# GpSimd in place of SyncE as issuer of the 16-row query and key copies in the first three units

## The chip, the cores and the metric

The kernel runs on one core of one Trainium2 chip. The metric is the device time of one execution in microseconds (us). Five engines work side by side, each through its own instructions in order: TensorE (PE; its weight loads are shown as PEld), VectorE (DVE), ScalarE (ACT), GpSimd (POOL) and SyncE (SP). They wait for each other by semaphores. An engine that issues a DMA hands the copy to the 16 DMA engines and goes on; the time that the issue itself takes on SP is shown as SPq.

## The reference

Three stages follow each other. A linear attention with a complex decay, per head, for 4 batches, 8 heads, 768 positions and a head width of 48:

```python
a_re_n, a_im_n = (a_re * scale, a_im * scale)       # scale = min(|a|, 0.999) / (|a| + 1e-6)
for t in range(S):
    new_re = ar * S_re - ai * S_im
    new_im = ar * S_im + ai * S_re
    S_re, S_im = (new_re + kv, new_im)              # kv = outer(k[t], v[t])
    y[:, :, t] = einsum('bhd,bhde->bhe', q[:, :, t], S_re)
```

Its output, 3072 tokens of 384 channels, goes through a dense layer `g = h * cos(h)` with `h = x @ w_in` and `g @ w_out` (2048 hidden channels), and then through a mixture of 8 experts of 1024 hidden channels: each token goes to the expert with the largest logit, and the result is scaled by two gates.

## The kernel before

The sequence is cut into chunks of 128 positions, and two chunks make a **unit**; there are 12 units (0 to 11). For each unit three things happen, pipelined over the units.

- **Scan** (`scan`, L377 and after). DVE forms the running products of the decay in `core` (tiles `t`, `l_t`, `pb`), their inverse in `inverse`, and normalises the next unit's decay in `normal` (the last large step is the product on `a_t`). `gates` is a run of small GpSimd instructions on `fg`, `eb` and `ne`.
- **`post`** multiplies queries and keys with the decay (`qkt`, in two parts r = 0 and 1, real and imaginary) and then brings them from the layout of the scan, channels over all 128 partitions, into the layout of the matmuls, 48 rows for each head and part: `out_` does it with five DMAs for each chunk and part into the tile `qkr`, all issued by SyncE: two copies of 48 rows (L372, heads 0 to 5), one of 32 rows (L373) and two of 16 rows (L375). The last three belong to heads 6 and 7, whose 48 channels lie in two places. A unit has two chunks and two parts, so 12 + 8 = 20 DMAs. At their end SP issues the load of the next `qk_t` (L229).
- **`attn`** computes the scores from `qkr` (PE L444, tile `sc`), masks them on DVE (`pt`), and adds the state: `s_` and its copy `ss` with the two halves swapped, which two more DMAs of SP make (L491, L492). `s_` and `ss` are multiplied with a column of `qkr` for all heads and added into `tp`; `pv_t` (L463, L468) gives the chunk's output, and `x` is its copy for the dense layer. The next chunk's state comes from PE `m` (L481).

The dense layer is `mm1` (L513), the cosine on ACT and DVE (`act2`, `act3`) and `mm2` (L577), eight steps for each unit; `evac`, `routing` and GpSimd's indirect scatters (L585) bring each token's row to its expert. In units 0 and 1 the weights of the dense layer are still being decoded, checked and multiplied (L706 to L755), on DVE, ACT and PE. After the last unit comes the mixture of experts, which is mostly PE.

A scheduler sets the order of each engine's instructions: it takes the program, simulates it with its own durations, and places what it believes ready first, by priority. So who issues a DMA changes not only that queue but also the order on the other engines. For each DMA the copies into `qkr` are told apart by region: scores of heads 0 to 3 wait for the 48-row copies alone, while the products `s_` and `ss` need the copies of all heads of their chunk in both parts.

Of the kernel before, what the change touches and what calls it, by code (L numbers as in the profile page):

```python
# [140 lines left out]
def build(tc, ap, out, force=False):  # L141
    nc = tc.nc
    V, A, G, PE, SY = nc.vector, nc.scalar, nc.gpsimd, nc.tensor, nc.sync
# [66 lines left out]
    def tt(e, o, a, b, op):  # L210
        return e.tensor_tensor(out=o, in0=a, in1=b, op=op)  # L211
# [16 lines left out]
    def load_qk(u):  # L228
        SY.dma_start(qk_t, ap["qk"][u])  # L229
# [129 lines left out]
    def put_gates():  # L359
        bc = [128, 2, NCOL, 2]  # L360
        A.copy(qkt[:, :, :, :, C], fg[:, 2, 0:1].unsqueeze(3).to_broadcast(bc))
        A.copy(qkt[:, :, :, :, C + 1], fg[:, 0].unsqueeze(3).to_broadcast(bc))

    def post(u):
        qkr_t[u] = [qkrp.tile([96, H, 2, QP], F32, name="qkr") for _ in range(UC)]

        def out_(cc, r):

            s = qkt[:, r, 3 * cc:3 * cc + 3].rearrange("p j k t -> p j (k t)")
            d = qkr_t[u][cc][48 * r:48 * r + 48].rearrange("d h k t -> d h (k t)")  # L370
            for i in range(2):
                SY.dma_start(d[:, i:6:2], s[48 * i:48 * i + 48])  # L372
            SY.dma_start(d[0:32, 6:8], s[96:128, 0:2])  # L373
            for i in range(2):
                SY.dma_start(d[32:48, 6 + i], s[96 + 16 * i:112 + 16 * i, 2])  # L375

        nc_ = UC if u < 1 else 1  # L377
        put_gates()
        for cc in range(nc_):
            c = slice(NCOL // nc_ * cc, NCOL // nc_ * (cc + 1))  # L380
            for r in range(2):
                n = NCOL // nc_
                mark["post", u] = tt(V, qkt[:, r, c, :, 0:C].rearrange("p c k t -> p k c t"),
                                     l_t[:, r:r + 1, c].to_broadcast([128, 2, n, C]), qk_t[:, :, c], MUL)
                yield
                for k in [cc] if nc_ == UC else range(UC):
                    out_(k, r)
        if u + 1 < NU:
            load_qk(u + 1)
        yield  # L390
# [872 lines left out]
    if True:  # L1263
# [34 lines left out]
        for u in range(NU):  # L1298
# [21 lines left out]
            for s in range(NS):  # L1320
# [6 lines left out]
                i = u * NS + s - 2  # L1327
# [60 lines left out]
```

## Time and profile before

| | us |
|---|---|
| median of 3 runs | 952.21 (951.52 to 952.86) |
| the profiled execution | 952.07 |
| its span on the core | 950.3 |
| PE busy | 867.6 |
| DVE busy | 659.0 |
| ACT busy | 571.8 |
| POOL busy | 142.0 |

The profile gives for each engine its instructions in order with start and duration, what ended the idle time ahead of them, and the chain of work that ended last. The profiled execution is 1.8 us longer than its span, which is time around the program on the core. From about 600 us on PE has hardly a gap; the units 0 to 2 lie in the first 215 us, where no engine is busy all the time.

### The profile page before, as it was taken

Reading aid. Unit: us, or ns where it says so; the run is one execution under the profiler, and the core shown is the slowest. Engines: PE = TensorE matmul, PEld = TensorE weight load, DVE = VectorE, ACT = ScalarE, POOL = GpSimd, SP = SyncE. Lnnn points to the kernel's source line nnn. Section 1 sums busy time; section 2 is a strip of 40 time slices with the busy share of each in tenths; the row PEclk is TensorE's granted clock in tenths of the full one; section 3 lists DMA queues with packets and bytes.
Section 4 is the critical chain, followed back from the end, with each engine's and each line's share of the span. In section 5 each row is a group of like instructions: output and inputs, shape, how many; then the busy total and the mean of one; then the engine's idle time right before and its main releaser. Section 6 shows DMA issues by size and latency. Waiting matters only on the chain.

```text
span 950.3 us, 18853 instructions
## 1 busy us (share of the span) xinstructions
PE 867.6 (91%) x7149; PEld 758.8 (80%) x7149; DVE 659.0 (69%) x1416; ACT 571.8 (60%) x1264; POOL 142.0 (15%) x246
## 2 busy tenths in 40 slices
PE   0477989979999799999999999899999999999997
PEld 0456677757777588888878889789899899999997
DVE  6988878887877698989888888444564454345521
ACT  7684976647665758676767766445764354355521
POOL 0000101021111222311312021101111110212111
PEclk9997999999999999999999999999999999999999
DMA  9813046337265544241415450341337552454100
GB/s 332 329 44 97 30 109 217 102 113 208 70 173 175 158 133 131 63 129 53 139 52 153 136 172 19 104 140 50 96 103 220 171 181 59 137 186 145 29 28 28
DMA packets 67206, 119.13 MB, mean 125 GB/s; under 512 B 12239, under 2 KB 44895, under 8 KB 66836
## 3 DMA queue, kind: packets, MB, share of 16 engines
q1 hardware_dynamic: 60132, 107.75, 36.5%
q0 software_dynamic: 6976, 10.10, 3.2%
q8 instruction: 58, 0.95, 0.4%
q14 instruction: 40, 0.33, 0.1%
HBM read 80.69 MB, written 26.77 MB: 113 GB/s over the span
## 4 chain that ended last, share of the span: by engine, by line
PE 40%; DVE 23%; ACT 13%; DMA 9%; issue 7%; SPq 6%; POOL 1%; DVEq 0%; ACTq 0%; POOLq 0%
PE h L965 10%; PE o L577 6%; PE h L513 6%; PE p L989 6%; PE p L981 4%; DVE qkt L211 4%; DVE t L211 3%; DMA qkr<-qkt 3%; DVE l_t L211 2%; DVE g L561 2%; SPq L375 2%; SPq L372 2%; DVE nt L211 2%; PE sc L444 2%; DVE pt L211 2%
## 5 line engine op out<-in xcount | busy, mean ns | idle before, releaser
L513 PE MATMUL h<-x,wi 128*128 128x256 f32 x1728 | 243.7, 292 | 10.5 <-DVE g L561 6.3
L513 PEld LDWEIGHTS h<-x,wi 128*128 128x128 f32 x1728 | 218.2, 192 | 25.3 <-DVE g L561 7.7
L577 PE MATMUL o<-wo,g 128*128 128x400 f32 x464 | 169.4, 505 | 1.9 <-DVE g L561 1.9
L577 PEld LDWEIGHTS o<-wo,g 128*128 128x128 f32 x464 | 83.6, 191 | 53.4 <-issue 2.7
L965 PE MATMUL h<-xe,w1t 128*128 128x384 f32 (+6 forms) x576 | 118.7, 349 | 0.0
L969 DVE SCALAR_TENSOR_TENSOR hh<-h,hh 128x384 fp32r<-128x384 f32 (+6 forms) x64 | 37.2, 582 | 117.5 <-ACT hh L968 117.5
L965 PEld LDWEIGHTS h<-xe,w1t 128*128 128x128 f32 x576 | 101.9, 188 | 5.2
L968 ACT ACTIVATE hh<-h 128x384 fp32r<-128x384 f32 (+6 forms) x64 | 32.8, 514 | 114.1 <-PE h L965 108.9
L521 ACT ACTIVATE g<-h 128x512 f32<-128x512 f32 x96 | 57.3, 597 | 52.0 <-PE h L513 52.0
L561 DVE SCALAR_TENSOR_TENSOR g<-g,h 128x512 f32<-128x512 f32 x96 | 65.4, 681 | 31.6 <-ACT g L523 31.4
L585 POOL DMA_INDIRECT xs<-rows,si x46 | 60.0, 1305 | 177.9 <-DVE si L632 58.1
L989 PE MATMUL p<-w2t,hh 128*128 128x384 f32 (+1 forms) x384 | 76.7, 343 | 0.0
L577 PE MATMUL o<-wo,gh 128*128 128x400 f32 x304 | 69.4, 350 | 0.0
L989 PEld LDWEIGHTS p<-w2t,hh 128*128 128x128 f32 (+1 forms) x384 | 66.0, 186 | 1.5 <-ACT hh L968 0.4
L523 ACT ACTIVATE g<-g 128x512 f32<-128x512 f32 x96 | 60.8, 633 | 2.1
L444 PE MATMUL sc<-qkr 96*128 96x128 f32 x384 | 56.1, 288 | 5.5 <-ACT rows L601 2.7
L522 ACT ACTIVATE g<-h 128x512 f32<-128x512 f32 x96 | 57.9, 603 | 1.8
L444 PEld LDWEIGHTS sc<-qkr 96*128 96x128 f32 x384 | 51.1, 199 | 9.7 <-issue 3.7
L211 POOL TENSOR_TENSOR fg<-l_t,m 128x12 f32<-128x12 f32 x24 | 5.9, 268 | 350.9 <-DVE l_t L211 236.2
L585 POOL DMA_INDIRECT out_dram<-o,tok x28 | 34.6, 1234 | 150.2 <-issue 56.1
L577 PEld LDWEIGHTS o<-wo,gh 128*128 128x128 f32 x304 | 53.3, 188 | 0.5
L555 ACT CAST gh<-g 128x512 fp32r<-128x512 f32 x38 | 23.4, 617 | 44.2 <-DVE g L561 44.1
(290 smaller groups left out, 1562.7 us busy)
## 6 DMA issues: line engine op xcount, KB each, us to landing
stg<-in_w_dram SPq DMA_DIRECT2D x32, 768.0 KB, 6.3
qkr<-qkt SPq DMA_DIRECT2D x96, 146.2 KB, 3.4
a_t<-in_a_dram SPq DMA_DIRECT2D x12, 768.0 KB, 5.3
qk_t<-in_qk_dram SPq DMA_DIRECT2D x12, 768.0 KB, 4.9
xs<-in_xz_dram SPq DMA_DIRECT2D x17, 401.0 KB, 8.2
vt<-in_v_dram SPq DMA_DIRECT2D x24, 256.0 KB, 2.6
raw<-in_w_in_dram SPq DMA_DIRECT2D x7, 768.0 KB, 12.9
raw<-in_w_out_dram SPq DMA_DIRECT2D x7, 768.0 KB, 15.8
```

The source lines that it names most:

```text
L211: return e.tensor_tensor(out=o, in0=a, in1=b, op=op)
L444: PE.matmul(sc[:, h], lhsT=t[:, h, 1, 0:C], rhs=t[:, h, 0, 0:C], start=True, stop=True)
L513: PE.matmul(h[:, i], lhsT=wis[s][:, wi, kk, i * 128:(i + 1) * 128], rhs=x_t[u][:, xi, kk], start=n == 0, stop=n == 8)
L521: A.activation(out=g, in_=h, func=AF.Square, accum_out=hck[:, u * NS + s:u * NS + s + 1])
L522: mark["sin"] = A.activation(out=g, in_=h, func=AF.Sin, scale=0.5)
L523: A.activation(out=g, in_=g, func=AF.Square, scale=float(np.sqrt(2.0)))
L561: V.scalar_tensor_tensor(out=g, in0=g, scalar=1.0, in1=hps.pop((u, s)), op0=SUB, op1=MUL)
L577: PE.matmul(o, lhsT=a[:, i, cs], rhs=w[:, i], start=s == 0 and n == 0 and i == 0, stop=s == NS - 1 and n == len(prods) - 1 and i == 1)
L585: sc = G.indirect_dma_start(in_offset=None, oob_is_err=False, **kw)
L965: PE.matmul(h, lhsT=w[:, wi, kk, f * 128:(f + 1) * 128], rhs=x[:, xi, kk], start=n == 0, stop=n == 8)
L981: PE.matmul(o2[e][d][:, 0:c], lhsT=w[:, wi, f, d * 128:(d + 1) * 128], rhs=hh[:, hi], start=f == 0 and n == 0, stop=f == KE - 1 and n == 2)
L989: mm = PE.matmul(o2[e][j][0:w_, 0:DM], lhsT=hh[:, hi, j * w_:(j + 1) * w_], rhs=w[:, wi, f], start=f == 0 and n == 0, stop=f == KE - 1 and ...
```

## The change

In units 0 to 2 the copies of 16 rows (L375) are issued by GpSimd; in units 3 to 11 SyncE goes on issuing them.

```diff
             for i in range(2):
-                SY.dma_start(d[32:48, 6 + i], s[96 + 16 * i:112 + 16 * i, 2])
+                (G if u < 3 else SY).dma_start(d[32:48, 6 + i], s[96 + 16 * i:112 + 16 * i, 2])
```

That is 8 DMAs for each of three units, 24 in all. On SyncE, here in unit 0, the end of the copies before (from the last chunk and part on):

```order
L372 DMA qkr<-qkt 48x3x260 x2
L373 DMA qkr<-qkt 32x520
L375 DMA qkr<-qkt 16x260 x2
L229 DMA qk_t<-in_qk_dram 128x1536
L491 DMA ss<-s__468 48x384
```

and now on GpSimd, between the gates of unit 0 (`fg`) and those of unit 1:

```order
L356 TENSOR_SCALAR fg<-fg 128x6
L357 COPY fg<-fg 128x6
L375 DMA qkr<-qkt 16x260 x8
L211 TENSOR_TENSOR fg<-l_t,m_131 128x12 x2
L348 COPY eb<-l_t 128x2x6
```

SP now goes from L373 to the next L372, or to L229, at once; nothing else stands between GpSimd's gates and the eight copies.

The order on the other engines moved with it. On PE in unit 0, from the transposes of keys on (`sc` are scores from `qkr`, `m` the state of the next chunk), before:

```order
L429 MATMUL m<-ident,qkt 128x128 x3
L481 MATMUL m<-vt,kn 32x48 x19
L444 MATMUL sc<-qkr 128x128 x2
L481 MATMUL m<-vt,kn 32x48 x4
L444 MATMUL sc<-qkr 128x128 x4
L481 MATMUL m<-vt,kn 32x48
L444 MATMUL sc<-qkr 128x128 x2
L481 MATMUL m<-vt,kn 32x48 x24
```

and now:

```order
L429 MATMUL m<-ident,qkt 128x128 x3
L444 MATMUL sc<-qkr 128x128 x6
L481 MATMUL m<-vt,kn 32x48 x8
L444 MATMUL sc<-qkr 128x128 x2
L481 MATMUL m<-vt,kn 32x48 x16
L444 MATMUL sc<-qkr 128x128 x4
```

The scores of chunk 0 moved ahead of its state; the third row from the end of the second list, two scores of heads 6 and 7, needs GpSimd's copies, and 16 matmuls of the state stand behind it.

On ACT, between the inverse of unit 2 (L250, L254, L255, L243) and its gates (L361), before:

```order
L254 ACT_TABLE_LOAD
L254 ACTIVATE qkt<-nt 128x768
L523 ACTIVATE g<-g 128x512
L255 ACTIVATE qkt<-qkt 128x768
L243 ACTIVATE a_t<-nt 128x768
L521 ACTIVATE g,hck<-h 128x512
L522 ACT_TABLE_LOAD
L522 ACTIVATE g<-h 128x512
L523 ACTIVATE g<-g 128x512
L361 COPY qkt<-fg 128x24
```

and now:

```order
L254 ACT_TABLE_LOAD
L254 ACTIVATE qkt<-nt 128x768
L601 ACTIVATE rows<-o_1069 128x400
L522 ACT_TABLE_LOAD
L522 ACTIVATE g<-h 128x512
L255 ACTIVATE qkt<-qkt 128x768
L243 ACT_TABLE_LOAD
L243 ACTIVATE a_t<-nt 128x768
L601 ACTIVATE rows<-o_1070 128x400
L523 ACTIVATE g<-g 128x512
L521 ACTIVATE g,hck<-h 128x512
L361 COPY qkt<-fg 128x24
```

A sine of the dense layer (L522) moved in between the functions of the inverse, and the table of functions is loaded twice more: once ahead of L243, and once more behind L361, where the next row is again a load for L522. On DVE the products of the state also moved ahead: in unit 1 `s_` with `ss` stands now ahead of the product on `a_t` and stood behind it, and in unit 2 it stands ahead of the first products `t` of the next scan, where five instructions of that scan stood ahead of it.

## Rows read from the trace of the kernel before

**Rows 1.** The page's part 4: the chain that ended last, by line.

```profile
PE h L965 10%; PE o L577 6%; PE h L513 6%; PE p L989 6%; PE p L981 4%; DVE qkt L211 4%; DVE t L211 3%; DMA qkr<-qkt 3%; DVE l_t L211 2%; DVE g L561 2%; SPq L375 2%; SPq L372 2%; DVE nt L211 2%; PE sc L444 2%; DVE pt L211 2%
```

**Rows 2.** Busy time in stretches: stretch, its length, busy us (instructions), clock, DMA.

```profile
122.00:150.00 28.00, 25.63 (x354) 22.04 (x354) 20.71 (x47) 17.70 (x52) 0.00 (x0) 0.94 0.42 110
150.00:172.00 22.00, 21.68 (x130) 17.21 (x130) 17.25 (x33) 18.12 (x36) 3.01 (x14) 1.00 0.60 213
...
360.00:405.00 45.00, 45.00 (x452) 39.18 (x451) 40.05 (x86) 31.92 (x75) 12.86 (x20) 1.00 0.36 106
```

**Rows 3.** Timeline of SP: start, us, engine, line, operation, tiles, count.

```profile
62.13 1.39 SPq L372 DMA_DIRECT2D qkr<-qkt  x2
...
64.21 1.22 SPq L375 DMA_DIRECT2D qkr<-qkt  x2
...
75.43 0.58 SPq L229 DMA_DIRECT2D qk_t<-in_qk_dram  x1
76.11 0.51 SPq L491 DMA_DIRECT2D ss<-s__468  x1
...
121.76 1.29 SPq L372 DMA_DIRECT2D qkr<-qkt  x2
...
171.15 1.33 SPq L372 DMA_DIRECT2D qkr<-qkt  x2
```

**Rows 4.** The chain in order of time, 55 to 215 us: start, us, what.

```profile
76.67 5.08 DMA ss<-s__468
```

**Rows 5.** Timeline of PE; in brackets the idle time ahead and what ended it.

```profile
85.13 0.65 PE L463 MATMUL pv_t<-qkr,tp 96*32 96x128 f32 x8 [5.77 <-DVE tp L211]
...
131.81 0.68 PE L444 MATMUL sc<-qkr 96*128 96x128 f32 x4 [0.41 <-DMA qkr<-qkt]
```

**Rows 6.** Timeline of DVE in units 0 to 2.

```profile
64.59 1.02 DVE L706 TENSOR_SCALAR raw<-raw 128x768 uint32<-128x768 uint32 x2
...
75.28 0.68 DVE L211 TENSOR_TENSOR pt<-sc,cb 128x512 f32<-128x512 f32 x1
...
80.06 0.96 DVE L211 TENSOR_TENSOR wi<-raw,wi 128x768 fp32r<-128x768 f32 x1 [1.56 <-ACT wi L727]
81.93 0.56 DVE L211 TENSOR_TENSOR s__468<-s__468,qkr 96x384 f32<-96x384 f32 x1 [0.91 <-DMA ss<-s__468]
...
129.56 1.76 DVE L211 TENSOR_TENSOR a_t<-a_t,nt 128x1536 f32<-128x1536 f32 x1
...
133.38 0.56 DVE L211 TENSOR_TENSOR s__549<-s__549,qkr 96x384 f32<-96x384 f32 x1 [0.87 <-DMA qkr<-qkt]
...
141.93 0.56 DVE L211 TENSOR_TENSOR s__888<-s__888,qkr 96x384 f32<-96x384 f32 x1 [1.31 <-DMA ss<-s__888]
...
180.21 0.63 DVE L211 TENSOR_TENSOR t<-a_t 128x192 f32<-128x192 f32 x2 [1.67 <-ACT a_t L291]
...
183.38 0.56 DVE L211 TENSOR_TENSOR s__969<-s__969,qkr 96x384 f32<-96x384 f32 x1 [1.50 <-DMA qkr<-qkt]
```

**Rows 7.** Timeline of GpSimd: indirect scatters, later in the kernel.

```profile
553.42 3.35 POOL L585 DMA_INDIRECT xs<-rows,si  x1 [0.30 <-issue]
...
601.40 0.97 POOL L585 DMA_INDIRECT xs<-rows,si  x1 [0.30 <-issue]
602.67 0.97 POOL L585 DMA_INDIRECT xs<-rows,si  x1 [0.30 <-issue]
```

**Rows 8.** DMA issues: tiles, issuer, count, KB each, median us from issue to landing.

```profile
qkr<-qkt SPq DMA_DIRECT2D x96, 16.2 KB, 2.3
...
xs<-rows,si POOLq DMA_INDIRECT x46, 3.4
```

**Rows 9.** Timeline of ACT in the inverse of unit 2.

```profile
158.02 1.47 ACT L250 ACTIVATE qkt<-l_t 128x1536 f32<-128x1536 f32 x1
...
161.43 1.28 ACT L254 ACT_TABLE_LOAD   x1
...
163.99 0.83 ACT L255 ACTIVATE qkt<-qkt 128x768 f32<-128x768 f32 x1
```

## The prediction

> **What bounds the kernel now.** I read the chain by line first: SP's issues of the 48-row and the 16-row copies stand in it with 2% each, and the copies into `qkr` with 3% [rows 1]. These shares run over all 12 units, so the question is what a shorter issue queue gives in units 0 to 2, and I read those stretch by stretch. The busy time per stretch says who could use an earlier copy: from 122 to 150 us PE is busy for 25.63 of 28 us, DVE for 20.71 and ACT for 17.70; from 150 to 172 us PE for 21.68 of 22; from 360 to 405 us for all of 45 [rows 2]. So behind the first units PE has almost no gaps, and a gain made early is kept to the end if it comes as PE work that starts earlier; there is little later into which it could vanish, and as little with which a loss could be made good. The gaps themselves are few. In unit 0 PE stands for 5.77 us until `tp` [rows 5], and DVE for 1.56 and 0.91 us, the latter until `ss` has landed [rows 6]. In unit 1 DVE waits 0.87 us for a copy into `qkr` and 1.31 us for `ss`, PE 0.41 us for a copy [rows 5, 6]. In unit 2 DVE waits 1.50 us for a copy [rows 6].
>
> **What leaves SP.** A pair of 16-row issues takes 1.22 us [rows 3], with the step to the next some 1.27. In unit 0 the 20 issues run from 62.13 to the start of the `qk_t` load at 75.43 [rows 3], 13.3 us. Without four pairs it is 13.3 - 4 x 1.27 = 8.2 us: SP is free 5.1 us earlier in each unit, and its second half of copies starts 2.5 us earlier. What gets faster is what queues behind them: `ss`.
>
> **What comes to GpSimd.** No direct copy issued by GpSimd is in this trace. The nearest rows are its indirect scatters, whose best rows take 0.97 us with 0.30 us ahead, one every 1.27 us (601.40, 602.67), and whose longest takes 3.35 [rows 7]. They land 3.4 us after issue, a 16-row copy of SP 2.3 us after [rows 8]. The scatters carry 128 rows and read an index, the copies 16 rows and none, so I take the short end, 1.28 us a copy, and 3.4 us to landing. From below SP's 0.61 us a copy would be a bound, from above 3.65. The GpSimd queue itself has nothing that waits behind the eight copies: the gates of the next unit follow, and in unit 0 they come more than 30 us later.
>
> **Unit 0.** The fourth copy, the last of chunk 0, is issued at 62.1 + 3 x 1.28 = 65.9 and lands at 69.3; the 16 state matmuls behind its scores then take well under 1 us, so `s_` can be there at about 71. SP is free for `ss` at 62.1 + 8.2 + 0.7 = 71.0 (before: 76.11 [rows 3]). The second half of `ss` was issued at 76.67 and landed 5.08 us later, with the `qk_t` load ahead of it [rows 4]; that load stays ahead, so I keep the 5.1: issue 71.6, landing 76.7. The last GpSimd copy lands at 62.1 + 7 x 1.28 + 3.4 = 74.5, earlier. DVE reaches `s_` behind the same instructions as before, at the end of the `pt` of 75.28, 75.9 [rows 6], waits until 76.8 and is 5.1 us ahead of 81.93 [rows 6]. Then stand `s_`, one `wi`, `ss`, `a_t`, `pt` and `tp`, by their rows 0.56, 0.96, 0.56, 1.76, 0.68 and 0.56, less 0.1 overlap each some 4.5 us: `tp` at 81.3, PE at 81.6 in place of 85.13 [rows 5]. PE gains 3.5 us. DVE gains only its idle time, 2.47 us less the 0.9 that stay, 1.6. The next post waits for both ACT and DVE work, so I take a value between: **-2.5 us** (from -3.5 to -1.6).
>
> **Unit 1.** SP starts at 121.76 [rows 3]. `s__549` needs GpSimd's first and third pair; the sixth copy goes at 121.8 + 5 x 1.28 = 128.2 and lands at 131.6, against 133.38 before [rows 6]. But the product on `a_t`, at 129.56 to 131.3 before [rows 6], now stands behind it: DVE comes to `s_` at about 129.5, stands until 131.6, and the scan of unit 2 gets its decay some 3 us later than before, counted from the start of the unit. Against that, `ss` for the next chunk, no longer behind SP's copies, and the scores come earlier: the waits of 0.87 and 1.31 us [rows 6] can go, and PE's 0.41 [rows 5]. PE has work without a gap after 131.81, so all of 2.6 us is the upper bound. I take **-0.5 us** (from -2.6 to +1.5).
>
> **Unit 2.** The same from 171.15 [rows 3]: the sixth copy lands at 171.2 + 5 x 1.28 + 3.4 = 181.0, against 183.38 [rows 6]. Before, DVE filled 1.7 us ahead of that wait with the first `t` from 180.21 [rows 6]; now `s_` stands ahead of them. The net is 2.4 - 1.7 = 0.7: **-0.7 us** (from -1.5, the whole wait, to +1.5).
>
> **The tables.** ACT loads its table twice more, 1.28 us each [rows 9], in a stretch in which it is busy for 18.12 of 22 us [rows 2]. L255, for which DVE waits, started 163.99 - 158.02 = 5.97 us after L250 [rows 9]; in the new order two table loads, not one, and other functions stand between, which by their durations makes 7.3 us. One load, **+1.3 us**, is in the way of unit 2; both would be 2.6, none 0, if DVE has other work there.
>
> The sum: -2.5 - 0.5 - 0.7 + 1.3 = -2.4 us. The profiled execution took 952.07 us, the median is 952.21, so no correction: 949.7. All good ends make -3.5 - 2.6 - 1.5 = -7.6, 944.5; all bad ones -1.6 + 1.5 + 1.5 + 2.6 = +4.0, 956.1.
>
> **A rule against the change.** The weights' L706 takes 0.5 us for 768 elements while a `wi` of the same size takes 0.96 [rows 6], so DVE runs it at about twice the rate; it stands at 64.59, where GpSimd issues. The Trainium skill, page SBUF — State Buffer, section SBUF: two separate sides, says that a DMA from GpSimd has its descriptors written by GpSimd, and that VectorE, in its two-port fast mode, locks GpSimd out meanwhile. By that rule the three L706 of unit 0 (two in the row, one after it) would hold the copies there for up to 1.5 us; units 1 and 2 have no such instruction on DVE at their copies, and no row of this trace shows a copy held in that way. With it the fourth copy would land at 70.8 instead of 69.3 and the sum would be about -1.5 us.
>
> **The rivals.** *More than that.* If a direct copy costs GpSimd 1.0 us or less and lands in 2.3 us as SP's do, the sixth copy lands 2.5 us earlier than I count, at 129 and 178.5; DVE does not stand in units 1 and 2, the scan is not pushed back, and the good ends hold with the tables paid: -7.6 + 1.3 = -6.3, 945.8. For it: 16 rows against 128. Against: the scatters' best rows do not fall below 0.97 [rows 7].
>
> *Nothing.* PE has no gap behind 131.81, so what unit 0 brings ahead may only lengthen a wait in unit 2, where the order now has two more table loads: -1.6 + 2.6, or the same plus a little: within 1.9 us of 952.2. For it: the 21.68 of 22 us [rows 2]. Against: the 5.77 us gap [rows 5] is real PE time.
>
> *Slower: a wait on GpSimd takes the place of the wait on SP.* The place is DVE at `s_` in units 1 and 2, where the scan's products stand behind it. `s__549` falls behind the 133.38 of before when 121.8 + 5p + 3.4 exceeds it, at p = 1.64 us a copy; in unit 2, with the 1.7 us that no longer fill the wait, at p = (183.4 - 1.7 - 3.4 - 171.2) / 5 = 1.42. At p = 2.3, between the best and the longest scatter, they land at 136.7 and 186.1: 3.3 us and 2.7 + 1.7 = 4.4 us lost, with the tables 1.3, against 2.5 gained in unit 0: +6.5, 958.7; at p = 1.8, +0.8, +1.9, +1.3 and -2.5, about +1.5. For it: a scatter of 3.35 us [rows 7]. Against: two in a row at 0.97.
>
> **How the numbers follow.** A measurement of this kernel can tell about 0.2%, 1.9 us, from no change: faster is below 950.3, slower above 954.1. I give the forecast 0.40 (a quarter of that falls within 0.2%), the larger gain 0.22, nothing 0.15, slower 0.23 (of which 0.03 stay within 0.2%). Faster: 0.30 + 0.22 = 0.52; same: 0.10 + 0.15 + 0.03 = 0.28; slower: 0.20. The forecast's own range, its good and bad ends, is 944.5 to 956.1; nearly 1 in 10 lies above 955.5 (the slow rival's far part) and as much below 944.
>
> **What would show it.** Right: SP's copies in each of the three units over in about 8 us; `ss` of unit 0 issued near 71 in place of 76.11; PE's gap before `tp` at 2 to 3 us in place of 5.77; GpSimd's copies 1.0 to 1.3 us apart; ACT's two extra table loads at the inverse of unit 2. Wrong: copies 1.6 us apart or more and a wait of DVE at `s_` of over 3 us in unit 1; or a gain that is there at 130 us and gone at 215, which would say that the tables or PE ate it; or a difference that only comes up after 215 us, where the order on PE and DVE moved too and which I count at nothing, since PE has no gap there to win or lose.

## The result and the profile after

The changed kernel takes 956.08 us (median of 5 runs, 954.25 to 960.34) against 952.21 (951.22 to 953.95): ratio 1.006, 95% interval 1.0038 to 1.0081 (the ratio on record is estimated from all the runs; the two medians alone give 1.004, inside the interval). It is slower by 3.9 us, where 949.7 was forecast. The profiled execution is the longest of the five (960.34 us, span 958.6); a second measurement on another chip gave 957.30 against 950.06, ratio 1.0071 (1.0053 to 1.0088).

What the change does to the two issuers came as forecast, or better. SyncE's timeline after, which answers to [rows 3]:

```profile
62.78 1.39 SPq L372 DMA_DIRECT2D qkr<-qkt  x2
...
70.96 0.59 SPq L229 DMA_DIRECT2D qk_t<-in_qk_dram  x1
74.81 0.52 SPq L491 DMA_DIRECT2D ss<-s__468  x1
...
121.12 1.29 SPq L372 DMA_DIRECT2D qkr<-qkt  x2
...
177.22 1.34 SPq L372 DMA_DIRECT2D qkr<-qkt  x2
```

From the first copy to the `qk_t` load it is 8.2 us, not 13.3 (in unit 1 8.4 for 14.3, in unit 2 9.1 for 14.1). GpSimd's timeline, and its landing row (least, median, longest):

```profile
63.40 4.41 POOL L375 DMA_DIRECT2D qkr<-qkt  x8 [12.85 <-ACT raw L755]
...
121.39 1.07 POOL L375 DMA_DIRECT2D qkr<-qkt  x2 [16.24 <-ACT qkt L362]
122.72 2.86 POOL L375 DMA_DIRECT2D qkr<-qkt  x6 [0.26 <-issue]
...
177.72 1.07 POOL L375 DMA_DIRECT2D qkr<-qkt  x2 [18.09 <-DVE qkt L211]
```

```profile
DMA to landing us min/median/max: 3.3/3.6/5.2
```

Eight copies take 4.41 us, 0.55 each, less than half of the 1.28 assumed from [rows 7]. Less time than was assumed, then; and yet the kernel is slower. The starts of the three units (the first row of each L372 group) tell where the time goes: 62.78, 121.12, 177.22, against 62.13, 121.76, 171.15 in [rows 3]. From unit 0 to unit 1 the kernel gains 1.3 us; from unit 1 to unit 2 it loses 6.7. A second step comes between units 3 and 4: they start at 222.24 and 270.94, against 215.93 and 260.62 before, so the lag grows there from 6.3 to 10.3 us; at the end of the span it is 8.3. Busy time in the stretches of [rows 2]:

```profile
122.00:150.00 28.00, 26.33 (x348) 22.42 (x349) 21.33 (x50) 15.64 (x49) 3.32 (x7) 0.94 0.53 122
150.00:172.00 22.00, 17.20 (x89) 13.53 (x88) 11.10 (x19) 16.42 (x31) 2.35 (x14) 0.87 0.55 198
...
360.00:405.00 45.00, 45.00 (x415) 39.53 (x414) 40.17 (x87) 33.51 (x73) 12.86 (x22) 1.00 0.33 97
```

Up to 150 us PE and DVE are even a little fuller than before (26.33 for 25.63 and 21.33 for 20.71; ACT, with 15.64 for 17.70, is not). From 150 to 172 us PE falls from 21.68 to 17.20, DVE from 17.25 to 11.10, and the granted clock from 1.00 to 0.87. Three engines stand for each other there. VectorE, which answers to [rows 6]:

```profile
78.13 0.55 DVE L211 TENSOR_TENSOR s__468<-s__468,qkr 96x384 f32<-96x384 f32 x1 [1.50 <-DMA ss<-s__468]
...
130.74 0.55 DVE L211 TENSOR_TENSOR s__549<-s__549,qkr 96x384 f32<-96x384 f32 x1 [1.90 <-DMA qkr<-qkt]
...
155.23 1.62 DVE L211 TENSOR_TENSOR l_t<-qkt 128x672 f32<-128x672 f32 x2
161.44 0.96 DVE L211 TENSOR_TENSOR nt<-qkt 128x768 f32<-128x768 f32 x1 [4.59 <-ACT qkt L250]
...
168.35 0.96 DVE L211 TENSOR_TENSOR nt<-nt,qkt 128x768 f32<-128x768 f32 x1 [5.08 <-ACT qkt L255]
```

ScalarE, for which it waits ([rows 9] before):

```profile
159.34 0.60 ACT L521 ACTIVATE g<-h 128x512 f32<-128x512 f32 x1 [3.10 <-PE h L513]
...
159.93 1.48 ACT L250 ACTIVATE qkt<-l_t 128x1536 f32<-128x1536 f32 x1
...
163.15 1.28 ACT L254 ACT_TABLE_LOAD   x1
...
165.70 1.28 ACT L522 ACT_TABLE_LOAD   x1
...
167.49 0.83 ACT L255 ACTIVATE qkt<-qkt 128x768 f32<-128x768 f32 x1
168.34 1.28 ACT L243 ACT_TABLE_LOAD   x1
...
170.38 0.49 ACT L601 ACTIVATE rows<-o 128x400 f32<-128x400 f32 x1
```

And TensorE, in unit 0 ([rows 5] before) and here:

```profile
68.49 2.90 PE L444 MATMUL sc<-qkr 96*128 96x128 f32 x12 [2.14 <-DMA qkr<-qkt]
...
84.14 0.43 PE L463 MATMUL pv_t<-qkr,tp 96*32 96x128 f32 x8 [4.31 <-DVE x L211]
...
154.86 0.88 PE L754 MATMUL h<-wg,rawr 128*128 128x16 f32 x6 [0.59 <-ACT rawr L752]
155.59 3.72 PE L513 MATMUL h<-x,wi 128*128 128x256 f32 x18
...
163.83 2.59 PE L513 MATMUL h<-x,wi 128*128 128x256 f32 x18
...
170.92 3.03 PE L577 MATMUL o<-wo,g 128*128 128x400 f32 x4 [3.15 <-ACT rows L601]
```

`l_t` is done at 156.85 us, earlier than in the kernel before, but L250, which reads it, stands on ScalarE behind an L521 that waits 3.10 us for TensorE's mm1, and that stands behind the last pairs of L751 and L754. Between L250 and L243 stand two L522, an L521, an L523, an L601 and three table loads, where before there was one load; L601, which empties the bank that TensorE's next L577 writes, comes last of all, and TensorE stands 3.15 us. It then goes on slowly: its four L577 take 3.03 us at a granted clock of 0.50 (170.9 to 174.0 us), where the kernel before has four L577 in 1.50. Likewise mm1's 18 matmuls took 3.72 us at 155.59, behind the stops for L752 and L755, at a clock of 0.57 (155.6 to 159.3), and 2.59 at 163.83, at 1.00 (163.8 to 166.4).

### The profile page after: what moved, and what is told of

It reads as the page before. It is cut to its first block, busy times and chain, and to the rows that moved or that the text cites. A ratio compares the mean times of both kernels' runs of the same rounds, so it can differ in the third digit from the quotient of the medians.

```text
span 958.6 us, 18912 instructions
## 1 busy us (share of the span) xinstructions
PE 874.2 (91%) x7149; PEld 766.5 (80%) x7149; DVE 658.0 (69%) x1416; ACT 576.6 (60%) x1266; POOL 153.3 (16%) x270
## 5 line engine op out<-in xcount | busy, mean ns | idle before, releaser
L513 PE MATMUL h<-x,wi 128*128 128x256 f32 x1728 | 246.9, 296 | 7.0 <-DVE g L561 5.9
L513 PEld LDWEIGHTS h<-x,wi 128*128 128x128 f32 x1728 | 222.3, 195 | 21.4 <-DVE g L561 7.4
L577 PE MATMUL o<-wo,g 128*128 128x400 f32 x464 | 171.4, 510 | 4.1 <-ACT rows L601 3.2
L577 PEld LDWEIGHTS o<-wo,g 128*128 128x128 f32 x464 | 85.0, 194 | 56.5 <-ACT rows L601 4.0
L521 ACT ACTIVATE g<-h 128x512 f32<-128x512 f32 x96 | 57.0, 594 | 54.7 <-PE h L513 52.0
L561 DVE SCALAR_TENSOR_TENSOR g<-g,h 128x512 f32<-128x512 f32 x96 | 65.3, 681 | 27.0 <-ACT g L523 26.1
L577 PE MATMUL o<-wo,gh 128*128 128x400 f32 x304 | 69.5, 350 | 0.0
L523 ACT ACTIVATE g<-g 128x512 f32<-128x512 f32 x96 | 60.7, 633 | 2.1
L522 ACT ACTIVATE g<-h 128x512 f32<-128x512 f32 x96 | 57.6, 600 | 1.9
L577 PEld LDWEIGHTS o<-wo,gh 128*128 128x128 f32 x304 | 53.3, 188 | 0.5
```

The costliest lines, as they stand in the source:

```text
L513: PE.matmul(h[:, i], lhsT=wis[s][:, wi, kk, i * 128:(i + 1) * 128], rhs=x_t[u][:, xi, kk], start=n == 0, stop=n == 8)
L521: A.activation(out=g, in_=h, func=AF.Square, accum_out=hck[:, u * NS + s:u * NS + s + 1])
L522: mark["sin"] = A.activation(out=g, in_=h, func=AF.Sin, scale=0.5)
L523: A.activation(out=g, in_=g, func=AF.Square, scale=float(np.sqrt(2.0)))
L561: V.scalar_tensor_tensor(out=g, in0=g, scalar=1.0, in1=hps.pop((u, s)), op0=SUB, op1=MUL)
L577: PE.matmul(o, lhsT=a[:, i, cs], rhs=w[:, i], start=s == 0 and n == 0 and i == 0, stop=s == NS - 1 and n == len(prods) - 1 and i == 1)
```

## The experiments: issuer against order

**Theory O**: the new issuer is cheap and good, and the loss is the order that the scheduler gave the three compute engines once the issuer was another. **Rival C**: GpSimd's copies themselves cost, since engines wait for their landing. They are told apart by giving one kernel's issuer the other's order. A and B are the lists of instruction names, engine by engine, of the changed kernel and of the kernel before; a list is forced by edges of issue order alone (no wait, no instruction is added), and SyncE and GpSimd are left to the scheduler:

```diff
-    p2_ctx.close()
+    p2_ctx.close(); follow(tc)
...
+def follow(tc):
+    by = {i.name: i for i in tc.nc.cur_bb.bb.instructions}
+    for names in ORDER.values():
+        ins = [by[n] for n in names if n in by]
+        for a, b in zip(ins, ins[1:]):
+            tc.add_manual_dep(b, a.name, NoSync, reason="order")
```

**1. The issuer alone**, the changed kernel with `ORDER = B`:

> The copies of units 0 to 2 are issued by GpSimd as in the changed kernel, but TensorE, VectorE and ScalarE execute their instructions in the order of the kernel before, word for word (32 table loads). Theory O (the loss is the new order of the engines): this kernel keeps what the shorter SyncE queue gives and is 1 to 3 us faster than before, ratio 0.997 to 0.999, unit 2's post step 1 to 2 us earlier than in before. Rival C (the copies themselves cost: VectorE stands at s_ and TensorE at the scores for GpSimd's slower transfers): it is as slow as the changed kernel, ratio 1.004 to 1.008. Rival N (neither alone): within 0.2% of before.

**2. The order alone**, the kernel before with `ORDER = A`:

> The complement: SyncE issues every copy, as before, and TensorE, VectorE and ScalarE execute in the order of the changed kernel, word for word (34 table loads). Theory O: the loss is all here, and since SyncE's queue is as long as before, it is as slow as the changed kernel or 1 to 3 us slower, ratio 1.005 to 1.010; L250 of unit 2's inverse runs behind L521 and two table loads, and unit 2's post step starts about 6 us later than before. Rival C: ratio 1.000 within 0.2%.

On one chip, where the kernel before took 955.31 us, the issuer alone takes 951.47, ratio 0.9959 (0.9937 to 0.9981), and the order alone 975.25, ratio 1.022 (1.0174 to 1.0266). Theory O holds, and rival C falls: with the old order GpSimd's copies are a gain. Under the new order they are a gain as well, 1.022 without them against 1.006 and 1.0071 with them, on other chips. What fits is that this order was made for a short SyncE queue; that is argued, not shown. What the edges do by themselves was not measured either, since no run forces on a kernel its own order; the nearest are experiments 4 and 15, the same issuer without edges and with them, 1.0005 and 0.9992, whose intervals overlap. VectorE in the order alone, where the copies come from SyncE:

```profile
136.21 0.55 DVE L211 TENSOR_TENSOR s__549<-s__549,qkr 96x384 f32<-96x384 f32 x1 [3.92 <-DMA qkr<-qkt]
...
194.94 0.55 DVE L211 TENSOR_TENSOR s__969<-s__969,qkr 96x384 f32<-96x384 f32 x1 [5.55 <-DMA qkr<-qkt]
```

**3. The changed kernel again**, beside the next three:

> The changed kernel once more, on the same chip as the three beside it, since the runs of before reached from 949.95 to 960.61 us on the last chip. Theory O (the loss is the new order) and its rivals all expect the ratio of the first measurement, 1.004 to 1.008.

1.0071, as told above. The chips differ: the median of before was 950.06, 950.01, 954.48, 955.31 and 955.39 us on five. A cost got by comparing ratios of two chips is therefore rough (0.6%, by experiment 18).

**4, 5. One unit alone**, with the order that the scheduler makes for it:

```diff
-                (G if u < 3 else SY).dma_start(
+                (G if u < 1 else SY).dma_start(
```

> Only unit 0's eight copies go to GpSimd (u < 1). The order of the three compute engines is that of before but for 6 of 1,096 places on ScalarE, 23 on VectorE and 80 on TensorE, all in unit 0, and 32 table loads. Theory O: what the prediction gave unit 0 remains, 1 to 3 us faster, ratio 0.997 to 0.999. Rival C: the state matmuls behind the scores and the later landing take it back, ratio 1.000 to 1.003.

1.0005 (0.9983 to 1.0026). And with `u == 1`:

> Only unit 1's eight copies go to GpSimd (u == 1). That alone moves 353 places on ScalarE from unit 1 on, and two table loads come with it (34). Theory O: slower than before although only eight copies moved, ratio 1.003 to 1.008, with unit 2's post step 4 to 8 us late. Rival C: a third of the changed kernel's loss at most, ratio 0.999 to 1.003.

0.9994 (0.9965 to 1.0023). As a time, theory O's expectation missed: this kernel has the two extra table loads too and is not slower. Its trace has the stretch of unit 2's inverse again, though, on VectorE and on TensorE:

```profile
167.35 0.96 DVE L211 TENSOR_TENSOR nt<-nt,qkt 128x768 f32<-128x768 f32 x1 [5.08 <-ACT qkt L255]
```

```profile
169.92 1.27 PE L577 MATMUL o<-wo,g 128*128 128x400 f32 x3 [3.35 <-ACT rows L601]
```

Unit 2 starts at 176.22 us, 5.1 late, and unit 11 at 601.49, 7.4 late (before: 171.15 and 594.13); the time is made good only in the last unit, where the orders differ as well. So this run does not show that the stretch is free. Experiment 8 takes the two loads away.

## The experiments: where the order loses

**6, 7. Cut at unit 2's post step.** GpSimd issues the copies of units 0 to 2 in all kernels from here to 14. At these places both orders have executed the same instructions:

```diff
+ORDER = {"PE": A["PE"][:661] + B["PE"][661:], "DVE": A["DVE"][:273] + B["DVE"][273:], "ACT": A["ACT"][:228] + B["ACT"][228:]}
```

> GpSimd issues the copies of units 0 to 2. The three compute engines follow the changed kernel's order up to the post step of unit 2 (ScalarE's first 228 places, VectorE's first 273, TensorE's first 661, the same sets of instructions in both orders), and the order of before from there on. Theory O-early (the loss is the new order at unit 2's inverse, about 156 to 177 us): it keeps the 6 us of that stretch, ratio 1.003 to 1.008, and unit 2's post step at 176 to 178 us. Rival O-late (the loss comes from the order after it, units 3 and on): as fast as with the whole order of before, ratio 0.994 to 0.999.

1.0021 (1.0008 to 1.0034). With A and B exchanged:

> The complement: the order of before up to the post step of unit 2, the changed kernel's order from there on, GpSimd issuing the copies of units 0 to 2. Theory O-early: the first stretch is saved and only the 3 to 4 us of 215 to 262 us are lost, ratio 0.998 to 1.002. Rival O-late: ratio 1.003 to 1.008.

1.0018 (1.0004 to 1.0033). Neither expectation of one place held: each part loses, and in total about alike.

**8 to 11. Single engines put back.** First ScalarE's 32 places around unit 2's inverse:

```diff
+ORDER = {**A, "ACT": A["ACT"][:181] + B["ACT"][181:213] + A["ACT"][213:]}
```

> The changed kernel with 32 instructions of ScalarE (its places 181 to 212, around unit 2's inverse) put back into the order of before, and nothing else: L250 runs after L523 of its step, L254 after L522 and L601, L361 after L523, and the table loads are 32 again. TensorE and VectorE keep the changed kernel's order. Theory O-early, in its narrow form (ScalarE's order there is the cause): unit 2's post step comes back from about 177 to 172 us and the time to 0.996 to 1.001 of before. If TensorE's order does it, or a later stretch: 1.003 to 1.008, as the changed kernel.

1.0089 (1.0072 to 1.0105): nothing is regained, though the two extra table loads are gone again. So taking the two loads away on ScalarE is not enough. On ScalarE the wait for mm1 has only grown:

```profile
161.84 0.60 ACT L521 ACTIVATE g<-h 128x512 f32<-128x512 f32 x1 [6.75 <-PE h L513]
```

Then TensorE's places 526 to 570 as well, then TensorE's scores of unit 2 (661 to 764) alone, then all of these:

> The changed kernel, with two stretches of its order put back: TensorE's places 526 to 570 (mm1 of the next unit's first two steps ahead of the last L754 pair, as before) and ScalarE's places 181 to 212 (as in act_32_places). The 32 places of ScalarE alone gave nothing, because L521 waited 6.75 us for TensorE's mm1. Theory: TensorE's and ScalarE's order at unit 2's inverse cost together what order_new_to_unit2 lost; with both put back unit 2's post step is at 170 to 173 us and the ratio to before falls from 1.007 to 1.000 to 1.004. Rival (the loss of the first part lies earlier, in unit 1's scores and states): stays at 1.006 to 1.009.

> The changed kernel with TensorE's places 661 to 764 put back: unit 2's 16 score matmuls (L444) run after 17 and more mm1 matmuls of the step instead of after 4. In order_new_from_unit2 they stood 2.51 us for the copies and then ran at half speed (3.27 us for 16). Theory: the second part of the loss is this early place of the scores; ratio from 1.007 to 1.002 to 1.005. Rival (VectorE's order, the routing's L211 among it, or the later pv_t): stays at 1.006 to 1.008.

> Both of the edits above in one kernel: 149 places of TensorE and 32 of ScalarE out of 8,048 go back to the order of before. If the two causes are the whole loss and add up, the issuer's own gain is left: ratio 0.995 to 0.999. If a part of the loss lies elsewhere: 0.999 to 1.004.

1.0105 (1.0069 to 1.0142), 1.0108 (1.0071 to 1.0146) and 1.0108 (1.0069 to 1.0147), on a chip on which the changed kernel itself was not run. All three miss what theory O expected, and nothing is regained; the intervals of the first two reach into what the rivals allow. TensorE in the first of them:

```profile
158.98 1.01 PE L513 MATMUL h<-x,wi 128*128 128x256 f32 x3 [3.94 <-DVE g L561]
```

The step's L561 stands on VectorE, still in the new order, behind the products of the scan. An order is one thing over three engines: with a piece of it on one, another waits.

**12, 13. The stretch of unit 2's inverse on all three engines**, put back in the changed kernel:

```diff
+ORDER = {"PE": A["PE"][:466] + B["PE"][466:571] + A["PE"][571:], "DVE": A["DVE"][:235] + B["DVE"][235:271] + A["DVE"][271:], "ACT": A["ACT"][:179] + B["ACT"][179:213] + A["ACT"][213:]}
```

> The changed kernel with one stretch of its order put back on all three compute engines together: TensorE's places 466 to 570, VectorE's 235 to 270, ScalarE's 179 to 212, about 144 to 175 us, that is unit 2's inverse with the last steps of unit 0's experts and the first of unit 1's beside it. Putting back single engines made it slower, since VectorE's L561 for the step ahead then stood behind the scan (TensorE idle 3.94 us at mm1 for it). Theory (this stretch is the whole first part of the loss): unit 2's post step is back at 168 to 171 us and the ratio falls from 1.007 to 1.000 to 1.004. Rival (the loss hangs on what stands ahead of or behind the stretch): 1.005 to 1.012.

1.0042 (1.0021 to 1.0063). It loses the whole second part still, so a value near experiment 7's was to come; it is a little above the range at its middle, and the post's L361 of unit 2 comes at 169.27 us, not 171.85. With A and B exchanged, this stretch alone is new:

> The complement: GpSimd issues the copies of units 0 to 2, the order of before everywhere but in that stretch (97 places of TensorE, 31 of VectorE, 28 of ScalarE differ), which has the changed kernel's order and its 34 table loads. Theory: this stretch alone costs the 5 to 6 us of order_new_to_unit2, ratio 1.000 to 1.004, against 0.996 of issuer_alone. Rival: the stretch costs nothing by itself, ratio 0.994 to 0.998.

1.0034 (1.0007 to 1.0062), where the issuer with the old order has 0.9959; both chips' before were within 1 us. So this stretch costs by itself some 0.75%, 7 us (some 4 to 11 by the two intervals, and over two chips). On the first chip, that of this run, the two halves of the issuer with the old order come to 0.9958 together (experiments 15 and 16), which bears the comparison out. Its trace takes 55.56 us from unit 1 to unit 2, where experiment 1's takes 50.16; of these 5.4 us 3.5 are left at the start of unit 11. The rows of the changed kernel are there again, in a kernel that is the old one up to 144 us. VectorE:

```profile
160.70 0.96 DVE L211 TENSOR_TENSOR nt<-qkt 128x768 f32<-128x768 f32 x1 [5.22 <-ACT qkt L250]
...
167.61 0.96 DVE L211 TENSOR_TENSOR nt<-nt,qkt 128x768 f32<-128x768 f32 x1 [5.08 <-ACT qkt L255]
```

**14. The stretch behind unit 2's post step**, new by itself:

```diff
+ORDER = {"PE": B["PE"][:661] + A["PE"][661:834] + B["PE"][834:], "DVE": B["DVE"][:273] + A["DVE"][273:332] + B["DVE"][332:], "ACT": B["ACT"][:228] + A["ACT"][228:256] + B["ACT"][256:]}
```

> GpSimd issues the copies of units 0 to 2, with the order of before everywhere but in the stretch behind unit 2's post step (about 176 to 215 us: TensorE's places 661 to 833, VectorE's 273 to 331, ScalarE's 228 to 255), which has the changed kernel's order: the 16 score matmuls behind 4 mm1 matmuls and VectorE's s_ product ahead of the scan's first products. Theory: the engines stand there for GpSimd's copies (TensorE 2.51 us, VectorE 3.25 us in order_new_from_unit2) and this stretch makes most of the second half of the loss: ratio 0.999 to 1.003, against 0.996 of issuer_alone. Rival (the second half of the loss lies in units 3 and 4 and later): 0.994 to 0.998.

1.0021 (1.0007 to 1.0035), in total as much as experiment 7 lost (1.0018, before at 950.0 us on both chips). That units 3 and later add nothing does not follow: by the traces experiment 14 loses further between units 2 and 3 (48.73 us, for 44.78 in experiment 7), where TensorE stops for 5.59 us at the end of the stretch in the new order, and experiment 7 between units 3 and 4 (48.11 us, for 45.13 here and 44.69 in the kernel before). TensorE, VectorE and SyncE in this kernel:

```profile
178.83 3.75 PE L444 MATMUL sc<-qkr 96*128 96x128 f32 x16 [2.53 <-ACT a_t L291]
...
215.68 2.71 PE L513 MATMUL h<-x,wi 128*128 128x256 f32 x11 [5.59 <-DVE x L211]
```

```profile
179.43 0.55 DVE L211 TENSOR_TENSOR s__969<-s__969,qkr 96x384 f32<-96x384 f32 x1 [2.87 <-DMA qkr<-qkt]
```

```profile
173.92 1.99 SPq L372 DMA_DIRECT2D qkr<-qkt  x2
175.96 0.71 SPq L373 DMA_DIRECT2D qkr<-qkt  x1
```

Between the last transposes and the scores stand, in the old order, 16 mm1 matmuls and a step's mm2, and now four mm1 matmuls: TensorE stops for 2.53 us; the 16 then take 3.75 us, at a granted clock of 0.50 (178.8 to 182.6 us). The first of them read heads 0 to 3 alone, that is the 48-row copies of SyncE; those of the second half are issued only 4.2 us after the post's first (173.92 against 169.76), the last of them at 175.31, and a 48-row copy lands 3.4 us after its issue, by the median of the kernel before: at about 178.7, an estimate, and TensorE goes on at 178.83. GpSimd's copies are needed from the third matmul of the second tile on. So the engine stands here for what SyncE still issues, not for what was moved (the profile names ScalarE's L291, which ends at 178.80; in experiment 3 TensorE resumes at the same place while L291 runs, and a copy is named). VectorE needs both kinds and goes on at 179.43. All of GpSimd's copies had landed by 178.42; SyncE's 32-row copy, the row at 175.96, was issued last, so VectorE too stands for SyncE. In the changed kernel itself TensorE's stop at this place is absent in the first profile and 1.44 us in experiment 3's, and VectorE waits 3.24 and 2.68 us at `s__969`. Which wait carries the second part of the loss there stays open.

## The experiments: what the issuer is worth

**15, 16. By unit, with the old order**: `u < 1`, then `u in (1, 2)`, with `ORDER = B`.

> GpSimd issues unit 0's eight copies only, and the three compute engines keep the order of before, word for word. The prediction's unit 0 term, -2.5 us (-3.5 to -1.6): ratio 0.9963 to 0.9983. If TensorE waits for the later landing (2.14 us at L444 in the changed kernel) and takes it back: 0.999 to 1.002.

0.9992 (0.9969 to 1.0014), -0.8 us. VectorE and TensorE in unit 0:

```profile
80.47 0.96 DVE L211 TENSOR_TENSOR wi<-raw,wi 128x768 fp32r<-128x768 f32 x1 [1.29 <-ACT wi L727]
81.35 0.55 DVE L211 TENSOR_TENSOR s__468<-s__468,qkr 96x384 f32<-96x384 f32 x1
```

```profile
84.55 0.65 PE L463 MATMUL pv_t<-qkr,tp 96*32 96x128 f32 x8 [5.04 <-DVE tp L211]
```

The wait of 0.91 us for `ss` [rows 6] is gone, that for ScalarE's `wi` ahead of it stays, and `tp` moves little: TensorE's gap is 5.04 in place of 5.77.

> GpSimd issues the copies of units 1 and 2 only, with the order of before. The prediction's terms for units 1 and 2 were -0.5 and -0.7 us with a copy at 1.28 us; with the 0.5 us a copy that the chip showed they can be -1.5 to -3: ratio 0.997 to 0.9985. If the rival of the prediction holds (VectorE waits at s_ for GpSimd's later copies): 1.000 to 1.003.

0.9966 (0.9944 to 0.9988), -3.2 us; 0.9992 x 0.9966 = 0.9958, the 0.9959 of experiment 1. In experiment 1 TensorE's stop at the mm2 of unit 2's end ran as the first row here, and in the kernel before as the second:

```profile
200.34 2.96 PE L577 MATMUL o<-wo,g 128*128 128x400 f32 x8 [0.46 <-DVE g L561]
```

```profile
202.39 4.65 PE L577 MATMUL o<-wo,g 128*128 128x400 f32 x8 [1.89 <-DVE g L561]
```

With the earlier copies VectorE loses its 1.50 us at `s__969` [rows 6] and comes earlier to L561; the eight matmuls behind the short stop take 2.96 us at a granted clock of 1.00 (200.0 to 203.3 us), those behind the long one 4.65 at 0.64 (202.3 to 207.0). ScalarE's L361 of unit 3 stands at 209.25 us, not 212.70.

**17, 18. All twelve units, old order**, twice:

```diff
-                (G if u < 3 else SY).dma_start(
+                G.dma_start(
```

> GpSimd issues the 16-row copies of all twelve units, and the three compute engines keep the order of before, word for word. If what issuer_alone gained (ratio 0.996) is the shorter SyncE queue, the other nine units can give something too where a wait for qkr ends last, ratio 0.985 to 0.996; if it was unit 0's alone, 0.995 to 0.998; if the copies collide with GpSimd's scatters (3.35 us each from unit 3 on), 0.998 to 1.010.

948.79 us against 955.39, ratio 0.9934 (0.9909 to 0.9958).

> all_units_old_order once more, beside a kernel of the same chip, since the runs of before spread by 1% from chip to chip and within one: if the gain of the version that beat both kernels is real, the ratio is 0.990 to 0.996 again; if it came with that chip, 0.996 to 1.000.

937.73 us against 950.01, ratio 0.9875 (0.9857 to 0.9894), on another chip, with four runs; that is below both expected ranges. It is faster than the kernel before on both chips (the changed kernel was not run on them). TensorE is busy for 151.54 of the 160 us from 170 to 330 us, where the kernel before has 144.12:

```profile
170.00:330.00 160.00, 151.54 (x1370) 119.16 (x1369) 132.50 (x280) 101.42 (x234) 44.47 (x83) 0.97 0.56 160
```

## Why the prediction was wrong

**The step that failed** is the price of the new order. What moved after 215 us the prediction counts at nothing, "since PE has no gap there to win or lose", and of what moved at unit 2's inverse it prices one table load, +1.3 us. The runs showed in its place that the order costs about 1% and outweighs the issuer's gain: the issuer with the old order is at 0.9959, the stretch of unit 2's inverse in the new order alone costs some 7 us (experiment 13), and behind it the new order costs again (experiments 7 and 14). The terms one by one:

**SyncE's queue: right.** 8.2 us were forecast; 8.2, 8.4 and 9.1 came, against 13.3, 14.3 and 14.1.

**GpSimd's price: too high.** Taken at 1.28 us a copy from scatters [rows 7]; 0.55 was measured, below even SyncE's 0.61, which had stood as the bound from below. The landing of 3.4 us was right (3.6). Of the larger-gain rival's condition (1.0 us or less to issue, 2.3 to land) the first half thus held, and with the old order its direction did.

**Unit 0, -2.5: too large.** With the old order it is -0.8 by the runs (-3.0 to +1.3, so the size is not excluded) and -1.1 by the trace: TensorE's first mm1 result reaches ScalarE at 93.92 us with the start at 61.84, against 94.41 with 61.19, each by L361 ahead and the L521 behind. In the changed kernel's order unit 1 starts 1.3 us sooner after unit 0 than before, about half of the 2.5. There `s_` was to be there at 71 us and `ss` issued at 71.0; it was issued at 74.81. The step that failed here is "the 16 state matmuls behind its scores take well under 1 us". By themselves they do (0.70 us), but the scores ahead of them waited 2.14 us for copies, and on TensorE four more scores and 32 matmuls of `m` stand behind them until 74.28; only then, at 74.31, does ScalarE copy `m` into `s_`, which `ss` reads:

```profile
71.95 1.22 PE L444 MATMUL sc<-qkr 96*128 96x128 f32 x4
73.11 1.17 PE L481 MATMUL m<-vt,kn 128*32 128x48 f32 x32
```

That `ss` was in use 2.75 us after its last issue (75.38 to 78.13), not 5.1, made up for most of this: `tp` starts at 82.21 us, 81.3 was forecast. But TensorE's gap is 4.31, not 2 to 3, since it also waits for VectorE's `x`.

**The rule on VectorE locking GpSimd out**: in unit 0, with L706 on VectorE beside them, eight copies took 4.41 us, in unit 1, with none, two and six took 1.07 + 2.86 = 3.93 (4.19 with the gap between them). So at most 0.2 to 0.5 us can be a lock, not the 1.5 that the prediction estimated from L706's own times; no run here shows in which mode L706 runs, so why so little was held stays open. The Trainium skill, page SBUF — State Buffer, section SBUF: two separate sides, states that GpSimd cannot write a DMA's descriptors while VectorE runs an instruction in its two-port mode.

**Units 1 and 2, -1.2 together: too small at its middle** with the old order: -3.2, with an interval of -5.3 to -1.1 that just reaches the -1.2. The copies were priced too high, and the time that TensorE loses at the lower clock behind a long stop (the two L577 rows above, 4.65 and 2.96 us) was not counted. In the changed kernel's order the terms do not exist as they were put.

**The tables, +1.3: size right, place too narrow.** L255 starts 7.56 us after L250 where 7.3 was said. But L250 itself starts 1.9 us later than before although its input came 1.0 us earlier, L601 holds TensorE for 3.15 us, and the post is 6.1 us late. The sum priced one of the two loads of the new order at that place and did not walk what stands around them: what L521 there waits for, and who waits for L601. Experiment 13 shows what the stretch costs, and experiment 8 that nothing is regained when ScalarE alone is put back and the two loads go.

**"PE has no gap" and the order on from unit 2.** That TensorE was busy for 21.68 of 22 us [rows 2] was read as a stretch in which little can be lost. It is a property of that order: the new one left 4.8 us idle there. And behind 172 us, up to 360, [rows 2] has no row; in the kernel before TensorE does stop there, for instance here, and from 170 to 330 us it is busy for 144.12 of 160:

```profile
211.76 0.97 PE L513 MATMUL h<-x,wi 128*128 128x256 f32 x6 [2.82 <-ACT x L472]
```

The moved scores of unit 2 were looked at on VectorE alone, not on TensorE (experiment 14). Two signs were named in the prediction, and both came: a gain that is there at 130 us is gone at 177, and a further difference comes up after 215 us, the 4.0 us between units 3 and 4.

**The range.** 956.08 lies just inside the forecast's own range, whose bad end is 956.1. That is luck: the bad end is made of VectorE waiting for GpSimd's copies and of two table loads, and neither is what cost the time.

**The slower rival** had the right side with another mechanism. VectorE does stand at `s_` (1.90 us in unit 1, until 130.74), but GpSimd's last copy had landed at 129.06, so it stood for SyncE's; the rival's threshold, 1.42 to 1.64 us a copy, was never near, and the loss came from order.

## What to carry to other kernels

Where a scheduler sets the order, a small edit is two edits, and the second can be the larger: here the issuer gives 0.4% and the order takes about 1%, by ratios from several chips. Compare the built orders of all engines before pricing the edit, and at each place that moved ask on every engine what the instruction now ahead waits for; if the new order is worse, keep the old one and the edit both. Here an order could be put back with a gain only in stretches that begin and end with the same instructions done on every engine; a piece of it on one or two engines regained nothing.

## What the hardware showed that was not expected

GpSimd issues a small direct copy in 0.49 us (0.48 to 0.77, 24 copies), quicker than SyncE's 0.59 for the same copy, while its landing takes 3.6 us against 2.3.

A difference between chips has a place. On three chips the kernel before took 954.5 to 955.4 us, and in 11 of the 12 profiles taken there (all but unit1_only's) TensorE stops for nothing that the profile names, in the last unit's attention from 585 to 650 us and for 1.3 to 3.6 us in all; in the six profiles taken on the two chips at 950 us there is no such stop. The longest two in issuer_alone:

```profile
599.22 0.28 PE L481 MATMUL m<-vt,kn 128*32 128x48 f32 x4 [1.18 <-issue]
600.82 0.24 PE L481 MATMUL m<-vt,kn 128*32 128x48 f32 x1 [1.32 <-issue]
```

Experiments 17 and 18 are one kernel on a chip of either kind. Unit 11 starts at 580.24 us in both. Then the first has such stops, 2.66 us in all up to 591 us, and a granted clock of 0.91 and 0.74 (580.2 to 590, 590 to 600), where the second has none and 1.00. The mm1 behind them, in the first and in the second:

```profile
591.25 4.14 PE L513 MATMUL h<-x,wi 128*128 128x256 f32 x18
```

```profile
585.75 2.38 PE L513 MATMUL h<-x,wi 128*128 128x256 f32 x18
```

At the last scores the first is 7.2 us behind, of the 7.9 by which the two spans differ (943.9 and 936.0). So traces of two chips are better compared at the start of unit 11: there the issuer with the old order is 4.0 us ahead of the kernel before, the changed kernel 8.9 and 7.5 behind, the order alone 17.5 behind. These are single executions. What stops TensorE there was not tested.
